# Weight transfers on a second queue, and nine feed ticks ahead of the first attention head instead of three

## The chip, the cores and the metric

One core of a Trainium2 chip. The metric is the device time of one execution in microseconds (us). A core has the engines TensorE (PE), VectorE (DVE), ScalarE (ACT), GpSimd (POOL) and SyncE (SP), which run their own instruction streams in order and wait for one another by semaphores, and DMA engines that move data between memory and the core. Both SP and ACT issue transfers in this kernel.

## The reference

Attention of 4 batches with 8 heads, 576 positions and 64 columns a head, and on its 2304 rows of 512 values two gated layers, one after the other, each with weights of 512x2048 and 2048x512:

```python
scores = scale * np.matmul(q, k.transpose(0, 1, 3, 2))
cum = np.cumsum(np.maximum(s, 0.0), axis=-1)
bias = -(cum[:, :, :, None] - cum[:, :, None, :])
scores = np.where(causal, -1000000000.0, scores + np.minimum(bias, 0.0))
attn = np.exp(scores - max); attn = attn / (sum + 1e-09)
x = np.matmul(attn, v)                    # to [2304, 512]
h = x @ w_in;  x = (h * np.clip(h + 3.0, 0.0, 6.0) / 6.0) @ w_out
h = x @ w_in2; out = (h * (1.0 / (1.0 + np.exp(-h)))) @ w_out2
```

The weights arrive as float64.

## The kernel before

**Heads and steps.** A head is 256 queries ("A") or the other 320 ("B") of one head of one batch; the work runs in slots, and a slot has the parts of up to three heads in flight: scores on PE, the masked maximum on DVE (L534), the exponential on ACT (L552), transposes on PE copied by ACT (`thA`, L120) and the product with v. Slots 0 to 8 have heads alone: the first block of rows is complete after eight heads. From slot 9 on each slot also has a step of the first gated layer: `first` (L260 to L262) multiplies a chunk of w_in, `gate_high` puts the gate through ACT (L272) and DVE (L273), `second` (L299 to L301) multiplies a chunk of w_out. "Gate n" below is the n-th L273 of DVE; the rows of the block itself come by `xh` (ACT, L725).

**Weights.** The first layer's weights are 32 chunks, i0, o0, i1, o1 to i15, o15. Each is loaded as raw 64-bit words, 128x1024 of 32 bits, 512 KB (L147, `rawi`, `rawo`), and turned into a pair of float32 pieces by seven operations: ACT L159 and L160, POOL L161, DVE L172 and L176 (the join), ACT L120 (`CAST wi` or `wo`, the high piece) and DVE L187 (the low piece). `Feed.tick` drives them as a pipeline: a tick loads one chunk, does L159 to L161 of the chunk loaded three ticks before, the join of the one before that, and the high and low piece of the one before that. Three ticks run ahead of the slots; slots 0 to 8 then get 0.4 tick each, later ones 2. `split_rows` builds rows for later heads and stores them with six transfers to `rows_d` (L365).

**Order.** A scheduler sets the order of instructions on each engine from the program; the engines keep that order. All transfers of the two queues take their completion semaphores in turn from one set of eight, in the program's order over both queues.

Of the kernel before, what the change touches and what calls it, by code (L numbers as in the profile page):

```python
# [11 lines left out]
I32 = mybir.dt.int32  # L12
# [15 lines left out]
def kernel(  # L28
# [15 lines left out]
    nc = tc.nc  # L44
# [85 lines left out]
    class Chunk:  # L130
        def __init__(self, kind, m, f):
            self.key = (kind, m, f)
            self.src = ((w1i, w1o), (w2i, w2o))[m][kind == "o"][f]
            self.nm = f"{kind}{m}_{f}"
            self.home = wpool, f"{kind}{f}"
# [2 lines left out]
            pool, tag = self.home  # L138
            return pool.tile(shape, dt, tag=tag, name=f"{name}{self.nm}")

        def load(self):
            if self.src.dtype == F32:
                self.val = self.place([P, DM], F32, "raw")
                nc.sync.dma_start(self.val, self.src)
            else:
                raw = self.place([P, 2 * DM], I32, "raw")
                nc.sync.dma_start(raw, self.src.bitcast(I32))  # L147
                words = raw.rearrange("p (n two) -> p n two", two=2)
                self.words = words[:, :, 0], words[:, :, 1]

# [38 lines left out]
    class Feed:  # L189


        def __init__(self, keys, hi_eng, lo_eng):
            self.ch = [Chunk(*k) for k in keys]
            self.hi_eng, self.lo_eng = hi_eng, lo_eng
            self.t = 0

        def done(self):
            return self.t >= len(self.ch) + 3 + 2

        def tick(self):  # L200
            n = len(self.ch)
            t = self.t - 3
            lo = self.lo_eng[t % len(self.lo_eng)] if 0 <= t - 2 < n else ""
            if lo:
                self.ch[t - 2].high(self.hi_eng[t % len(self.hi_eng)])
            if 0 <= t < n:
                self.ch[t].fields()
            if lo == "p":
                self.ch[t - 2].low(lo)
            if 0 <= t - 1 < n:  # L210
                self.ch[t - 1].join()
            if lo == "v":
                self.ch[t - 2].low(lo)
            if self.t < n:
                self.ch[self.t].load()
            self.t += 1


# [133 lines left out]
    def split_rows():  # L352

        def row(tag, name):
            return wpool.tile([BH, S], F32R, tag=tag, name=name)

        f = NF - 1
        hi, lo = row(f"i{f}", "cumh"), row(f"o{f}", "cuml")
        one, neg = row(f"i{NF // 2 - 2}", "one"), row(f"i{NF // 2 - 1}", "neg")
        nc.gpsimd.memset(f32(one), 1.0)  # L360
        nc.gpsimd.memset(f32(neg), -1.0)
        nc.scalar.copy(hi, crow)
        nc.vector.tensor_tensor(out=lo, in0=crow, in1=f32(hi), op=ALU.subtract)
        for r, t in enumerate((one, one, hi, lo, neg, neg)):
            nc.sync.dma_start(f32(rows_d[:, r, :]), f32(t))  # L365
# [347 lines left out]
    def split1(blk):  # L713

        n = sizes[blk][1]
        b, a, _ = blocks[blk][0]
        xhs, xls = [], []
        for c in range(NDC):
            xh = xpool.tile([P, n], F32R, tag=f"xh{c}", name=f"xh{blk}_{c}")
            xl = xpool.tile([P, n], F32R, tag=f"xl{c}", name=f"xl{blk}_{c}")  # L720
            srcs = [((xB if a else xA)[b, c], slice(0, T1))]
            if n > T1:
                srcs += [(xZ[c], slice(T1, n))]
            for src, o in srcs:
                nc.scalar.copy(xh[:, o], src)  # L725
                nc.vector.tensor_tensor(
                    out=xl[:, o], in0=src, in1=f32(xh[:, o]), op=ALU.subtract
                )
            xhs.append(xh)
            xls.append(xl)  # L730
        xsplit[blk] = [(xhs, xls)]
# [46 lines left out]
    feed = Feed([(kd, 0, f) for f in range(NF) for kd in "io"], "a", "v")  # L778
# [3 lines left out]
    def ticks(n):  # L782
        for _ in range(n):
            if not feed.done():
                feed.tick()
# [79 lines left out]
    def at(i):  # L865
        return heads[i] if 0 <= i < len(heads) else None


    loaded = 2
    for hd in heads[:loaded]:  # L870
        hd.load()
    ticks(3)
    for hd in heads[:loaded]:
        hd.load_cum()
    nc.sync.dma_start(pair_d, pairs)
    heads[0].places()
    k = 0
    p1 = p2 = None
    plan = [(True, False)] * (H + 1) + [(i < 55, True) for i in range(68)]
    nslot = 0  # L880
    for has_head, has_step in plan:
        cur = at(k) if has_head else None
        nx = at(k + 1) if has_head else None
        loads = []
        while has_head and loaded < len(heads) and loaded <= k + (
            2
        ):
            loads.append(heads[loaded])
            loaded += 1
        k += has_head and cur is not None  # L890
        tk = [0, 0, 0, 0]
        if not feed.done():
            rate = ((0.4,)*9+(2,))[min(nslot, len(((0.4,)*9+(2,))) - 1)]
            for i in range(4):
                feed_at += rate / 4
                tk[i] = int(feed_at)
                feed_at -= tk[i]
        slot(cur, p1, p2, nx, loads, has_step, tk)
        if nslot == 9:
            split_rows()  # L900
        p1, p2 = cur, p1
        nslot += 1
        if nslot == H + 1:
            p2.av_sum()
            p2 = None
            split1(0)
            turns["s"] = turns["s"][:1]
        if has_step and step in first_step[1:NB1]:
            blk = first_step.index(step)
            assert k - (cur is not None) >= (blk + 1) * H  # L910
            if p2:
                p2.av_sum()
                p2 = None
            if blk == NB1 - 1:
                cx.close()
                xpool = cx.enter_context(
                    tc.tile_pool(name="xlast", bufs=1, side="right", reuse_waits="tile")
                )
            split1(blk)
            if blk == NB1 - 1:  # L920
                break
# [70 lines left out]
    feed = Feed([("o", 1, f) for f in range(NF)], "a", "v")  # L992
# [293 lines left out]
```

## Time and profile before

| what | value |
|---|---|
| median of 3 runs | 1000.1 us (998.52 to 1000.47) |
| profiled execution | 1000.54 us, its span 998.8 us, granted PE clock 0.995 |
| busy share of the span | PE 97%, PEld 89%, DVE 74%, ACT 51%, POOL 32% |

The span is the time from the first to the last instruction in the trace; the shares are over the whole of it. The slots with heads alone end at 43 us and the last gate of the first sixteen steps is at 154 us, so the stretch that the change touches is the first sixth of the span.

### The profile page before, as it was taken

What the parts mean: (1) busy time and instruction counts of PE and PEld (TensorE: products, weight loads), DVE (VectorE), ACT (ScalarE), POOL (GpSimd) and SP (SyncE); (2) the same over time, 40 slices, a digit from 0 to 9 for tenths busy, and PEclk for the clock granted to TensorE, in tenths of its full rate; (3) what the DMA queues carried; (4) which work ended last, traced back from release to release, by engine and by line L of the source; (5) the groups of instructions that cost most, each with busy time, mean ns of one, the idle gap of its engine ahead of it and who ended that gap; (6) DMA issues with size and microseconds to landing.
All of it is one profiled execution on the core that took longest, in us unless ns stands there. A gap on an engine that the chain in (4) does not pass through costs nothing.

```text
span 998.8 us, 17929 instructions
## 1 busy us (share of the span) xinstructions
PE 970.8 (97%) x6268; PEld 891.6 (89%) x6268; DVE 737.9 (74%) x1757; ACT 511.0 (51%) x1177; POOL 317.2 (32%) x323
## 2 busy tenths in 40 slices
PE   8899989999999999999999999999999999999997
PEld 5789979999999999999997877899988989889996
DVE  6899998888789888988866799887574434743343
ACT  6898554555455555555446656564443323432332
POOL 4457853443333443434425566532000000000000
PEclk9999999999999999999999999999999999999999
DMA  5796112312222223222215957434354233442421
GB/s 174 225 302 198 47 40 67 92 46 63 83 77 75 71 59 92 60 64 80 60 39 186 392 212 237 163 116 190 133 195 169 77 145 110 167 154 76 148 74 64
DMA packets 54419, 125.41 MB, mean 126 GB/s; under 512 B 12332, under 2 KB 34076, under 8 KB 51000
## 3 DMA queue, kind: packets, MB, share of 16 engines
q1 hardware_dynamic: 53880, 123.60, 37.3%
q8 instruction: 50, 0.82, 0.3%
q10 hardware_dynamic: 448, 0.66, 0.2%
q14 instruction: 41, 0.34, 0.1%
HBM read 99.52 MB, written 24.69 MB: 124 GB/s over the span
## 4 chain that ended last, share of the span: by engine, by line
PE 70%; DVE 11%; DMA 8%; issue 4%; POOL 4%; SPq 3%; ACT 1%; POOLq 0%; DVEq 0%; ACTq 0%
PE a L1083 6%; PE a L1084 6%; PE a L1085 6%; PE h L1066 5%; PE h L1068 5%; PE h L1067 5%; PE ph L260 4%; PE ph L261 4%; PE ph L262 4%; PE acc L299 4%; PE acc L300 4%; PE acc L301 4%; PE poB L672 4%; DMA rawi<-in_w1i_dram 3%; POOL rawo L161 2%
## 5 line engine op out<-in xcount | busy, mean ns | idle before, releaser
L260 PE MATMUL ph<-xh,wi 128*128 128x256 f32 (+1 forms) x512 | 154.1, 303 | 3.2 <-DVE g L273 3.1
L300 PE MATMUL acc<-gl,wo 128*128 128x256 f32 (+1 forms) x512 | 151.1, 297 | 2.4 <-DVE gl L280 2.4
L261 PE MATMUL ph<-xl,wi 128*128 128x256 f32 (+1 forms) x512 | 151.6, 296 | 0.0
L262 PE MATMUL ph<-xh,wi 128*128 128x256 f32 (+1 forms) x512 | 151.3, 296 | 0.0
L301 PE MATMUL acc<-gh,wo 128*128 128x256 f32 (+1 forms) x512 | 149.8, 294 | 0.0
L1125 ACT ACTIVATE gh<-h 128x384 fp32r<-128x384 f32 x96 | 50.3, 524 | 185.4 <-DVE h L1133 185.3
L299 PE MATMUL acc<-gh,wo 128*128 128x256 f32 (+1 forms) x512 | 143.8, 297 | 0.0
L1083 PE MATMUL a<-wo,gh 128*128 128x512 f32 x288 | 113.5, 394 | 1.4 <-ACT gh L1125 0.9
L1084 PE MATMUL a<-wo,gh 128*128 128x512 f32 x288 | 113.1, 393 | 0.0
L260 PEld LDWEIGHTS ph<-xh,wi 128*128 128x128 f32 x512 | 97.4, 190 | 8.9 <-DVE g L273 2.5
L300 PEld LDWEIGHTS acc<-gl,wo 128*128 128x128 f32 x512 | 96.4, 188 | 6.4 <-DVE gl L280 3.5
L262 PEld LDWEIGHTS ph<-xh,wi 128*128 128x128 f32 x512 | 97.6, 191 | 3.0
L261 PEld LDWEIGHTS ph<-xl,wi 128*128 128x128 f32 x512 | 97.5, 190 | 3.2
L301 PEld LDWEIGHTS acc<-gh,wo 128*128 128x128 f32 x512 | 96.5, 189 | 3.3
L299 PEld LDWEIGHTS acc<-gh,wo 128*128 128x128 f32 x512 | 95.6, 189 | 3.4
L161 POOL TENSOR_SCALAR rawi<-rawi 128x512 int32<-128x512 f32 x32 | 70.0, 2188 | 74.1 <-ACT magi L160 48.4
L1085 PE MATMUL a<-wo,gl 128*128 128x512 f32 x288 | 90.0, 392 | 0.0
L161 POOL TENSOR_SCALAR rawo<-rawo 128x512 int32<-128x512 f32 x32 | 74.5, 2329 | 48.0 <-ACT mago L160 46.3
L1127 DVE TENSOR_TENSOR gl<-h,gh 128x384 fp32r<-128x384 f32 x96 | 53.8, 560 | 39.9 <-ACT h L1126 38.2
L114 POOL TENSOR_SCALAR gh<-g 128x512 fp32r<-128x512 f32 x68 | 50.6, 745 | 92.6 <-DVE g L273 77.4
L1133 DVE TENSOR_TENSOR h<-h,u 128x384 f32<-128x384 f32 x72 | 40.1, 557 | 53.5 <-PE h L1068 53.2
L1066 PE MATMUL h<-x0t,w 128*128 128x384 f32 x192 | 64.9, 338 | 0.7 <-DVE u L1133 0.7
(220 smaller groups left out, 2554.6 us busy)
## 6 DMA issues: line engine op xcount, KB each, us to landing
w<-w_d SPq DMA_DIRECT2D x18, 1792.0 KB
w_d<-w SPq DMA_DIRECT2D x8, 1792.0 KB
k2B<-in_kT_dram SPq DMA_DIRECT2D x64, 144.0 KB
rawi<-in_w1i_dram SPq DMA_DIRECT2D x16, 512.0 KB
rawo<-in_w1o_dram SPq DMA_DIRECT2D x16, 512.0 KB
rawi<-in_w2i_dram SPq DMA_DIRECT2D x16, 512.0 KB
rawo<-in_w2o_dram SPq DMA_DIRECT2D x16, 512.0 KB
q2B<-in_qT_dram SPq DMA_DIRECT2D x64, 80.0 KB
```

What stands on the lines that cost most here:

```text
L161: nc.gpsimd.tensor_scalar(out=high, in0=f32(high), scalar1=0.0, scalar2=float(SIGN), op0=ALU.is_lt, op1=ALU.mult,)
L260: nc.tensor.matmul(o, wih[:, cs], xh[c], start=c == 0, stop=False)
L261: nc.tensor.matmul(o, wih[:, cs], xl[c], start=False, stop=False)
L262: nc.tensor.matmul(o, wil[:, cs], xh[c], start=False, stop=c == NDC - 1)
L299: nc.tensor.matmul(a, woh[:, cs], gh[:, jj, :], start=b0, stop=False)
L300: nc.tensor.matmul(a, woh[:, cs], gl[:, jj, :], start=False, stop=False)
L301: nc.tensor.matmul(a, wol[:, cs], gh[:, jj, :], start=False, stop=b1)
L1066: nc.tensor.matmul(ps, w[:, 0, cs], xh[:, c, :], start=c == 0, stop=False)
L1083: nc.tensor.matmul(accs[t], gh[:, k, cs], woh, start=b0, stop=False)
L1084: nc.tensor.matmul(accs[t], gh[:, k, cs], wol, start=False, stop=False)
L1085: nc.tensor.matmul(accs[t], gl[:, k, cs], woh, start=False, stop=b1)
L1127: nc.vector.tensor_tensor(out=gl[:, i, o], in0=g, in1=f32(gh[:, i, o]), op=ALU.subtract)
```

## The change

`Chunk.load` takes the queue that issues its transfer, and `Feed` keeps one. It is ACT's queue from the start to the end of slot 8, and SP's after that. The three ticks ahead of the slots move ahead of the loads of the first two heads, and three more ticks follow the store of `pair_d`. `split_rows` comes after slot 7 instead of slot 9. Lines behind the edit stand 1 to 4 further down in the changed kernel.

```diff
--- before.py
+++ after.py
@@ -138,13 +138,13 @@
             pool, tag = self.home
             return pool.tile(shape, dt, tag=tag, name=f"{name}{self.nm}")
 
-        def load(self):
+        def load(self, queue=nc.sync):
             if self.src.dtype == F32:
                 self.val = self.place([P, DM], F32, "raw")
-                nc.sync.dma_start(self.val, self.src)
+                queue.dma_start(self.val, self.src)
             else:
                 raw = self.place([P, 2 * DM], I32, "raw")
-                nc.sync.dma_start(raw, self.src.bitcast(I32))
+                queue.dma_start(raw, self.src.bitcast(I32))
                 words = raw.rearrange("p (n two) -> p n two", two=2)
                 self.words = words[:, :, 0], words[:, :, 1]
 
@@ -193,6 +193,7 @@
             self.ch = [Chunk(*k) for k in keys]
             self.hi_eng, self.lo_eng = hi_eng, lo_eng
             self.t = 0
+            self.queue = nc.sync
 
         def done(self):
             return self.t >= len(self.ch) + 3 + 2
@@ -212,7 +213,7 @@
             if lo == "v":
                 self.ch[t - 2].low(lo)
             if self.t < n:
-                self.ch[self.t].load()
+                self.ch[self.t].load(self.queue)
             self.t += 1
 
 
@@ -867,12 +868,14 @@
 
 
     loaded = 2
+    feed.queue = nc.scalar
+    ticks(3)
     for hd in heads[:loaded]:
         hd.load()
-    ticks(3)
     for hd in heads[:loaded]:
         hd.load_cum()
     nc.sync.dma_start(pair_d, pairs)
+    ticks(3)
     heads[0].places()
     k = 0
     p1 = p2 = None
@@ -896,11 +899,12 @@
                 tk[i] = int(feed_at)
                 feed_at -= tk[i]
         slot(cur, p1, p2, nx, loads, has_step, tk)
-        if nslot == 9:
+        if nslot == 7:
             split_rows()
         p1, p2 = cur, p1
         nslot += 1
         if nslot == H + 1:
+            feed.queue = nc.sync
             p2.av_sum()
             p2 = None
             split1(0)
```

What the scheduler makes of it shows at three places. The first is ACT's start, up to the first exponential (`pb0A_0`). Before:

```order
L350 ACT_TABLE_LOAD
L350 COPY pairs<-orow 32x256
L362 CAST cumh<-orow 32x576
L159 ACTIVATE rawi_0_171<-rawi_0_171 128x512
L160 ACTIVATE magi_0_257<-rawi_0_171 128x512
L159 ACTIVATE rawo_0_173<-rawo_0_173 128x512
L160 ACTIVATE mago_0_354<-rawo_0_173 128x512
L159 ACTIVATE rawi_1_175<-rawi_1_175 128x512
L160 ACTIVATE magi_1_450<-rawi_1_175 128x512
L552 ACTIVATE pb0A_0_181,sums_127<-pb0A_0_181,mxA_0_180 128x128
```

And now, where nine transfers are issued by ACT (the L147 rows):

```order
L147 DMA rawi_0_163<-in_w1i_dram 128x1024
L147 DMA rawo_0_165<-in_w1o_dram 128x1024
L147 DMA rawi_1_167<-in_w1i_dram 128x1024
L351 ACT_TABLE_LOAD
L351 COPY pairs<-orow 32x256
L147 DMA rawo_1_184<-in_w1o_dram 128x1024
L159 ACTIVATE rawi_0_163<-rawi_0_163 128x512
L160 ACTIVATE magi_0_180<-rawi_0_163 128x512
L147 DMA rawi_2_192<-in_w1i_dram 128x1024
L159 ACTIVATE rawo_0_165<-rawo_0_165 128x512
L160 ACTIVATE mago_0_186<-rawo_0_165 128x512
L147 DMA rawo_2_203<-in_w1o_dram 128x1024
```

Further on in the same stretch, from ACT's last issue to the first exponential:

```order
L147 DMA rawi_4_490<-in_w1i_dram 128x1024
L120 CAST wi_0_194<-magi_0_180 128x512
L363 CAST cumh<-orow 32x576
L159 ACTIVATE rawi_2_192<-rawi_2_192 128x512
L160 ACTIVATE mago_1_284<-rawo_1_184 128x512
L159 ACTIVATE rawo_2_203<-rawo_2_203 128x512
L120 CAST wo_0_282<-mago_0_186 128x512
L159 ACTIVATE rawi_3_291<-rawi_3_291 128x512
L120 CAST wi_1_384<-magi_1_196 128x512
L159 ACTIVATE rawo_3_393<-rawo_3_393 128x512
L160 ACTIVATE magi_2_386<-rawi_2_192 128x512
L553 ACTIVATE pb0A_0_206,sums_127<-pb0A_0_206,mxA_0_205 128x128
```

Before its first exponential ACT had three chunks' L159 and L160 each. Now it has the L159 of eight chunks, five L160, three casts and nine issues; the rows between these two pieces are the transfers o2, i3 and o3, L159 and L160 of i1, and the L159 of o1.

The second is SP's start. Before, rows 8 to 18, the raw chunks i0, o0, i1, and what SP issues behind them up to the first transfer of the fourth head (`inA_3`):

```order
L147 DMA rawi_0_171<-in_w1i_dram 128x1024
L147 DMA rawo_0_173<-in_w1o_dram 128x1024
L147 DMA rawi_1_175<-in_w1i_dram 128x1024
L423 DMA inA_0_163<-pairs 2x1x512
L423 DMA inA_1_167<-pairs 2x1x512
L875 DMA pair_d<-pairs 32x1024
L413 DMA inA_2_191<-in_qT_dram 64x256
L414 DMA inA_2_191<-in_kT_dram 64x256
L403 DMA inA_2_191<-in_v_dram 128x128
L423 DMA inA_2_191<-pairs 2x1x512
L413 DMA inA_3_218<-in_qT_dram 64x256
```

Now, from the second head's transfers to the same place:

```order
L414 DMA inA_1_173<-in_qT_dram 64x256
L415 DMA inA_1_173<-in_kT_dram 64x256
L404 DMA inA_1_173<-in_v_dram 128x128
L424 DMA inA_0_169<-pairs 2x1x512
L424 DMA inA_1_173<-pairs 2x1x512
L877 DMA pair_d<-pairs 32x1024
L414 DMA inA_2_216<-in_qT_dram 64x256
L415 DMA inA_2_216<-in_kT_dram 64x256
L404 DMA inA_2_216<-in_v_dram 128x128
L424 DMA inA_2_216<-pairs 2x1x512
L414 DMA inA_3_243<-in_qT_dram 64x256
```

The three raw loads have left SP, and the transfers of a head follow each other. In the program's order over both queues the first transfer of `inA_2` is the eighth after ACT's o2, that of `inA_3` the eighth after o3.

The third is the tenth chunk, o4. SP before, from the ninth head:

```order
L413 DMA inA_0_405<-in_qT_dram 64x256
L414 DMA inA_0_405<-in_kT_dram 64x256
L403 DMA inA_0_405<-in_v_dram 128x128
L423 DMA inA_0_405<-pair_d 2x512
L413 DMA inA_1_442<-in_qT_dram 64x256
L414 DMA inA_1_442<-in_kT_dram 64x256
L403 DMA inA_1_442<-in_v_dram 128x128
L147 DMA rawo_2_457<-in_w1o_dram 128x1024
```

SP now, from the last transfer of the tenth head:

```order
L424 DMA inA_1_475<-pair_d 2x512
L366 DMA rows_d<-one 32x576 x2
L366 DMA rows_d<-cumh 32x576
L366 DMA rows_d<-cuml 32x576
L366 DMA rows_d<-neg 32x576 x2
L414 DMA inA_2_533<-in_qT_dram 64x256
L415 DMA inA_2_533<-in_kT_dram 64x256
L404 DMA inA_2_533<-in_v_dram 128x128
L424 DMA inA_2_533<-pair_d 2x512
L147 DMA rawo_4_585<-in_w1o_dram 128x1024
```

And ACT now, around the first use of o4:

```order
L553 ACTIVATE pb0A_6_412,sums_131<-pb0A_6_412,mxA_6_411 128x128
L553 ACTIVATE pb1A_6_413,sums_131<-pb1A_6_413,mxA_6_411 128x256
L553 ACTIVATE pb0A_7_445,sums_133<-pb0A_7_445,mxA_7_444 128x128
L553 ACTIVATE pb1A_7_446,sums_133<-pb1A_7_446,mxA_7_444 128x256
L159 ACTIVATE rawo_4_585<-rawo_4_585 128x512
L160 ACTIVATE mago_4_693<-rawo_4_585 128x512
L120 COPY thA_4_400<-pt0A_4_396 128x384
L726 CAST xh_1_557<-xA_1_382 128x256
L120 COPY thA_5_433<-pt0A_5_429 128x384
L159 ACTIVATE rawi_5_628<-rawi_5_628 128x512
```

SP had a raw load for every one or two heads there. Now the six stores of `rows_d` and a whole eleventh head stand ahead of o4, the first raw chunk that SP loads, and on ACT the L159 of o4 stands ahead of what remains for the first gate: the copies `thA_4` and `thA_5` and the rows `xh_1`.

Counted from the same orders, the operations of conversion on either side of the gates:

| engine, lines | where | before | now |
|---|---|---|---|
| ACT, L159 | ahead of gate 0 | 8 | 21 |
| DVE, L172 L176 L187 | ahead of gate 0 | 20 | 44 |
| DVE, the same | gate 0 to gate 7 | 30 | 31 |
| DVE, the same | gate 7 to gate 11 | 24 | 21 |
| DVE, the same | gate 11 to gate 16 | 22 | 0 |

The matmuls between gate 0 and gate 16 are the same in both.

## Rows read from the trace of the kernel before

**Rows 1.** Windows: us, busy us (instructions) of each engine, clock, DMA share, GB/s.
```profile
12.76:42.41 29.65, 24.71 (x173) 20.00 (x172) 26.28 (x105) 25.24 (x80) 12.87 (x7) 1.00 0.63 180
43.10:80.80 37.70, 35.48 (x270) 33.60 (x271) 36.30 (x111) 35.12 (x87) 23.40 (x12) 0.95 0.93 290
80.80:111.00 30.20, 27.95 (x231) 26.67 (x231) 29.17 (x70) 22.73 (x55) 22.12 (x14) 1.00 0.44 138
111.00:154.30 43.30, 38.26 (x291) 35.60 (x291) 42.59 (x97) 24.38 (x58) 25.81 (x24) 0.96 0.17 44
150.00:200.00 50.00, 49.80 (x410) 49.17 (x411) 42.99 (x121) 25.00 (x65) 19.51 (x27) 1.00 0.27 79
```

**Rows 2.** Chain of work in the first 40 us: start, us, what.
```profile
5.81 5.79 DMA rawi<-in_w1i_dram
11.61 0.48 SPq L413
...
28.91 4.46 DMA rawo<-in_w1o_dram
```

**Rows 3.** Timeline of ACT up to gate 0: start, us, operation.
```profile
38.84 0.61 ACT L120 CAST wo<-mago 128x512 fp32r<-128x512 f32 x1
39.35 0.47 ACT L120 COPY thA<-pt0A 128x384 f32<-128x384 f32 x1
39.72 0.41 ACT L725 CAST xh<-xA 128x256 fp32r<-128x256 f32 x1
40.02 0.69 ACT L159 ACTIVATE rawo<-rawo 128x512 int32<-128x512 uint32 x1
40.60 0.66 ACT L160 ACTIVATE mago<-rawo 128x512 f32<-128x512 f32 x1
...
41.52 0.41 ACT L552 ACTIVATE pb0A<-pb0A,mxA 128x128 f32<-128x128 f32 x1
41.91 0.50 ACT L552 ACTIVATE pb1A<-pb1A,mxA 128x256 f32<-128x256 f32 x1
42.41 0.46 ACT L272 ACTIVATE g<-ph,half 128x256 f32<-128x256 f32 x1
```

**Rows 4.** Timeline of DVE, gate 0 and gate 16.
```profile
43.11 0.41 DVE L273 SCALAR_TENSOR_TENSOR g<-g,ph 128x256 f32<-128x256 f32 x1
...
154.29 0.69 DVE L273 SCALAR_TENSOR_TENSOR g<-g,ph 128x512 f32<-128x512 f32 x1 [0.27 <-ACT g L272]
```

**Rows 5.** Timeline of ACT up to the first exponential, and the chunk o1.
```profile
4.65 0.40 ACT L350 COPY pairs<-orow 32x256 f32<-32x256 f32 x1 [2.65 <-DVE orow L345]
...
12.20 0.65 ACT L160 ACTIVATE magi<-rawi 128x512 f32<-128x512 f32 x1
12.76 0.39 ACT L552 ACTIVATE pb0A<-pb0A,mxA 128x128 f32<-128x128 f32 x1
...
19.50 0.70 ACT L159 ACTIVATE rawo<-rawo 128x512 int32<-128x512 uint32 x1 [0.55 <-DMA rawo<-in_w1o_dram]
```

**Rows 6.** Timeline of SP's queue, issues.
```profile
15.90 0.43 SPq L147 DMA_DIRECT2D rawo<-in_w1o_dram  x1
...
16.71 0.48 SPq L413 DMA_DIRECT2D inA<-in_qT_dram  x1
...
18.84 0.47 SPq L413 DMA_DIRECT2D inA<-in_qT_dram  x1
...
35.41 0.78 SPq L365 DMA_DIRECT2D rows_d<-one  x2
```

**Rows 7.** Timeline of ACT near the end, a transfer that ACT issues.
```profile
991.49 0.39 ACTq L1107 DMA_DIRECT2D out_dram<-o  x1
```

**Rows 8.** Groups of DVE between gate 0 and gate 16, two of conversion's six.
```profile
L187 DVE TENSOR_TENSOR wi<-magi,wi 128x512 fp32r<-128x512 f32 x13 | 10.8, 831 | 0.0
...
L172 DVE SCALAR_TENSOR_TENSOR magi<-magi,rawi 128x512 int32<-128x512 int32 x12 | 8.2, 684 | 0.3 <-POOL rawi L161 0.2
```

## The prediction

> **What bounds the kernel now.** I read the shares first: PE is busy 97% of the span, so an edit far from it is worth nothing unless it makes PE wait. Then the windows, to see where PE does not run at its own rate [rows 1]. From 150 to 200 us PE does 410 matmuls in 50 us, 8.2 a us, and is busy all through: that is its rate when everything is there. From gate 0 to gate 16 it does 270 + 231 + 291 = 792 matmuls in 111.2 us [rows 1, 4]; at 8.2 a us they would take 96.6. So 14.6 us could be won there, and the reader sees by whom it is lost: DVE is busy 36.3 of 37.7, 29.2 of 30.2 and 42.6 of 43.3 us [rows 1]. DVE bounds the steps, and a good part of its work there is conversion of weights. Ahead of gate 0 nothing is full: between the first exponential and gate 0 ACT is busy 25.2 of 29.65 us and DVE 26.3 [rows 1]; ACT and DVE hand the heads to each other. Last I read the chain of the first 40 us, which is transfers: SP's issue at 11.61 us follows the landing of i1, issued at 5.81, and the next gap follows o2, issued at 28.91 and 4.46 us under way [rows 2]. In the order shown above, the issue at 11.61 (`inA_3`) is the eighth transfer after i1. So an issue waits until the transfer eight before it, whose semaphore it reuses, has landed; the issues behind it on its engine wait with it.
>
> **The change part by part: the delay of gate 0.** It loads nine chunks early on ACT's queue, converts more of them ahead of gate 0, and leaves less conversion for later. I follow ACT, with occupancies taken from start to start [rows 3]: L159 0.58 us, L160 0.56 (12.20 to 12.76) [rows 5], a cast 0.51, `thA` 0.37, `xh` 0.30, the exponentials 0.39 and 0.50.
>
> First exponential. ACT's copy of `pairs` starts at 4.65 us [rows 5] and stays near there, since it waits for `irow`, still SP's first transfer; three issues in front of it make it 5.1 at its end. Behind it come six issues, 13 of L159 and L160, three casts and the `cumh` cast. An issue by ACT shows once, 0.39 us [rows 7]; SP's take 0.43 for these very transfers [rows 6], which I take: 2.6. With 13 x 0.57 = 7.4, 3 x 0.51 = 1.5 and 0.6 the sum is 12.1, so the first exponential starts at about 17.3 instead of 12.76 us, 17.5 with a short wait of the i4 issue for i2. That is 4.7 us late.
>
> From there to the L159 of o4 stand 16 exponentials (7.1), five of L159 and L160 (2.8), six casts (3.1), four `thA` (1.5) and an `xh` (0.3): 14.8 us, so ACT reaches o4 at 32.3 us if DVE and PE keep up.
>
> When o4 is there depends on SP. Its first transfer of `inA_2` waits for o2 by the rule of eight. ACT issues o2 behind two issues and four conversion operations, 5.1 + 0.9 + 2.3 = 8.3 us; landing takes 3.6 us (15.90 issued, L159 at 19.50) [rows 5, 6] to 4.46 [rows 2], so `inA_2` starts at 12.3. Heads `inA_2` and `inA_3` are done at about 17.4, held a little by o3 and i4. The next six take 2.13 us each (16.71 to 18.84) [rows 6]: 30.2. The six stores to `rows_d`, which the earlier `split_rows` puts here, take 6 x 0.39 = 2.3 (two in 0.78) [rows 6]: 32.5. The eleventh head, 2.13: 34.7. Only then is o4 issued, to land at 38.3 to 39.2. **ACT stands still for about 6.5 us, from 32.3 to 39**, and behind it wait the next exponentials and the `thA` copies and `xh` of the first block's last heads, which gate 0 needs. DVE and PE have nothing of their own to go on with.
>
> From o4 to gate 0 ACT has ten exponentials (4.5), twelve L159 (7.0), six L160 (3.4), five casts (2.6), six `thA` (2.2) and three `xh` (0.9): 20.5 us, so gate 0 is at 39 + 20.5 = 59.5 on ACT, 42.41 before [rows 3]. A second count agrees: from o4 to i10, whose L159 stands just ahead of the gate, twelve chunks of 512 KB and some 0.8 MB of heads are 7.1 MB, 24.5 us at the 290 GB/s of the densest window [rows 1]; 34.7 + 24.5 is 59.2. **I take a delay of 17 us.** Bounds: no stall at all and ACT full, 17.5 + 14.8 + 20.5 = 52.8, or +10.4; the last 20.5 us at the 0.85 of the stretch of before [rows 1], 63.1, or +20.7.
>
> **What is given back.** Conversion on DVE between gate 0 and gate 16 falls from 76 operations to 52. The cheapest of the six groups is 0.684 us a piece, the dearest 0.831 [rows 8]; with the middle, 0.75, 24 of them are 18 us of DVE. But PE cannot go under 96.6 us, so at most 14.6 come back. And it matters where they are missing: to gate 11 DVE has 52 instead of 54, which is 1.5 us of a stretch that DVE fills. From gate 11 to gate 16 it has none instead of 22, 16.5 us less; DVE's 42.6 fall to 26.1, PE becomes the bound there, and its 291 matmuls take 35.5 us instead of 43.3: 7.8. **I take 9.3 us back**, bounds 1.5 + 0 (ACT or the heads hold those last steps) and 14.6. Past gate 16 PE is full in both and runs the same matmuls: nothing further changes hands.
>
> The rest costs nothing. The queue itself moves bytes and does not add any; the earlier `split_rows` is priced above; `places` and the idle matmuls at the start are the same.
>
> What the second queue is worth by itself: SP loses six raw issues ahead of the ninth head, 0.43 us each [rows 6], 2.6 us, and ACT gets them. Behind this stands a sentence of the Trainium skill ("DMA: Bandwidth & Descriptors", section "Issuing engines are not separate DMA queues"): transfers started by several engines share the same DMA engines, and this saves only the time a sequencer takes to issue them. By it the change would be worth some 2.6 us and no more; whether these transfers overlap more than before, no row here shows yet, and the long delay above is of order and semaphores, not of bandwidth.
>
> **The sum.** 998.8 + 17 - 9.3 = 1006.5 for the span; with the 1.7 us that lie around it (1000.54 against 998.8), 1008.2. The profiled execution is 0.4 above the median of the runs, so the runs should show about 1007.5.
>
> **Rivals.** *Faster.* If o4 and the chunks behind it land before ACT comes to them, gate 0 is at 52.8 (+10.4), and if DVE's relief then reaches every step, 14.6 come back: -4.2, or 996. The point that decides is SP's issue of o4: ahead of 28 us, against my 34.7. For it: three of the waits in the chain are for landings, and raw loads spread over two queues could land sooner than 4.46 us. Against it: the six stores and eleven heads stand ahead of o4 whatever the landing. *Even.* Gate 0 at 57 to 59.5 and nearly the whole 14.6 given back: within 2 us, about 1000. For it: conversion that is done early is work that DVE need not do later, and DVE bounds these steps by 96% and more [rows 1]. Against it: the missing work is at the end, more than PE can use. *Nothing given back.* The heads with steps pace the stretch past gate 11, through ACT and POOL or the transfers of `q2A` and `k2A` that now stand behind the raw loads on SP: +17 less 1.5, about 1015.5. Against it: ACT is busy 24.4 of 43.3 us there [rows 1]. *The issue time alone.* The scheduled order delays nothing because the chain of transfers shrinks by as much as ACT gains: -2.6, about 997.5. Against it: 21 chunks' L159 instead of 8 stand ahead of the gate.
>
> **How the numbers follow.** The forecast, 1007.5, has 0.6, and its own range is 1002.5 to 1013 (17 less 14.6 is +2.4; 20.7 less 7.8 is +12.9). Faster by the rival with o4 early 0.1, by issue time alone 0.05; even 0.15; nothing given back 0.1. The measurement tells about 0.2%, 2 us, from no change. Of the forecast's low end a little falls to the other sides: faster 0.16, same 0.17, slower 0.67. The range from 997 to 1014 leaves out the rival with o4 early and the one with nothing given back, 0.2 together.
>
> **What the changed profile would show.** The first exponential at about 17.5 us; SP's first transfer of `inA_2` at 12 to 13 us; ACT idle from about 32 to 39 us until o4 lands; gate 0 on DVE at about 60 us; no conversion after gate 11, PE full from there, and gate 16 some 8 us later than 154.29 [rows 4]. The forecast is wrong if ACT reaches o4 with o4 landed, if gate 0 comes before 57.7 us on DVE (43.1 + 14.6, where delay and the most that can come back are equal), or if PE still waits for DVE between gate 11 and gate 16.

## The result and the profile after

The changed kernel takes 1010.6 us (median of 4 runs, 1008.2 to 1012.0) against 1000.3 of the kernel before in the same comparison: a ratio of 1.0093, 95% interval 1.0069 to 1.0117. It is slower, as forecast (1007.5), by 10.3 us instead of 7.4, and inside the range. The profiled execution has a span of 1010.2 us, 11.4 more than before's 998.8.

The page of the changed kernel, busy time of each engine over the span, and the granted clock of PE in 40 slices of 25 us, in tenths:

```profile
PE 984.0 (97%) x6268; PEld 904.0 (89%) x6268; DVE 736.3 (73%) x1757; ACT 511.6 (51%) x1177; POOL 311.6 (31%) x323
...
PEclk7759999999999999999999999999999999999999
```

PE has the same 6268 instructions and 13 us more busy time; the first three slices say why: the clock was granted at 0.7, 0.7 and 0.5 there. The windows of the changed kernel, cut at its own first exponential, its L159 of o4, its gate 0 (on ACT, then on DVE), gates 7, 11 and 16, answer to [rows 1]:

```profile
19.67:42.31 22.64, 21.12 (x93) 17.16 (x94) 19.95 (x71) 15.99 (x50) 10.31 (x5) 0.59 0.42 117
42.31:65.28 22.97, 19.11 (x94) 16.41 (x94) 17.65 (x61) 20.55 (x53) 12.04 (x6) 0.71 0.97 332
66.16:104.11 37.95, 36.34 (x270) 34.76 (x271) 36.44 (x107) 32.21 (x81) 23.86 (x12) 0.92 0.44 144
104.11:132.12 28.01, 27.34 (x230) 26.37 (x229) 27.82 (x74) 17.67 (x43) 19.11 (x14) 1.00 0.20 57
132.12:164.48 32.36, 32.36 (x278) 32.19 (x277) 22.28 (x56) 14.77 (x36) 8.93 (x15) 1.00 0.14 39
```

In time these windows hold 270 + 230 + 278 = 778 matmuls between gate 0 and gate 16, where the kernel before has 792: the matmuls are the same, but 228 instead of 216 run ahead of gate 0.

The gates on DVE, which answer to [rows 4]:

```profile
66.16 0.41 DVE L274 SCALAR_TENSOR_TENSOR g<-g,ph 128x256 f32<-128x256 f32 x1
...
164.48 0.69 DVE L274 SCALAR_TENSOR_TENSOR g<-g,ph 128x512 f32<-128x512 f32 x1 [0.81 <-ACT g L273]
```

Gate 0 is 66.16 - 43.11 = 23.1 us late. From gate 0 to gate 16 it takes 98.3 us instead of 111.2, so 12.9 come back; behind gate 16 it is 1.2 us more (845.7 against 844.5). 23.1 - 12.9 + 1.2 is the 11.4. Most of what comes back does so where it was forecast, from gate 11 to gate 16: 32.4 us instead of 43.3, with PE busy for all of it and DVE for 22.3 instead of 42.6.

Now how gate 0 came to be so late. ACT's timeline, answering to [rows 3, 5]; behind an operation stand the idle time ahead of it and what ended it:

```profile
6.08 0.40 ACT L351 COPY pairs<-orow 32x256 f32<-32x256 f32 x1 [2.63 <-DVE orow L346]
...
13.07 0.62 ACT L120 CAST wi<-magi 128x512 fp32r<-128x512 f32 x1 [1.04 <-DMA rawi<-in_w1i_dram]
...
16.36 0.62 ACT L120 CAST wo<-mago 128x512 fp32r<-128x512 f32 x1 [0.41 <-DVE mago L176]
...
19.67 0.39 ACT L553 ACTIVATE pb0A<-pb0A,mxA 128x128 f32<-128x128 f32 x1
...
33.53 0.62 ACT L120 CAST wo<-mago 128x512 fp32r<-128x512 f32 x1 [1.76 <-DVE sums L562]
...
37.31 0.41 ACT L726 CAST xh<-xA 128x256 fp32r<-128x256 f32 x1 [1.09 <-DVE xA L122]
...
39.91 0.40 ACT L553 ACTIVATE pb0A<-pb0A,mxA 128x128 f32<-128x128 f32 x1 [1.16 <-DVE xtA L695]
...
42.31 0.68 ACT L159 ACTIVATE rawo<-rawo 128x512 int32<-128x512 uint32 x1
...
65.28 0.46 ACT L273 ACTIVATE g<-ph,half 128x256 f32<-128x256 f32 x1
```

The first exponential is at 19.67 us, 2.2 later than forecast. `irow`, issued at 0.73 us in both kernels, landed later beside the raw loads, so the copy of `pairs` starts at 6.08 instead of 4.65. Then ACT waited for landings and for DVE's joins. The wait ahead of 13.07 is that of an issue, by the rule of eight: i4 goes out when i2 has landed, as the chain of work and ACT's timeline have it:

```profile
6.52 6.10 DMA rawi<-in_w1i_dram
...
12.64 0.33 ACTq L147 DMA_DIRECT2D rawi<-in_w1i_dram  x1
```

From the first exponential to o4 it took 22.6 us instead of the 14.8 that ACT's own work would need. The operation ahead of the row at 42.31 ends at 42.18 and o4 lands at 42.28, so ACT waits for it for some 0.1 us. The stall of 6.5 us for o4 does not exist, because ACT comes 10 us later than forecast; o4 itself lands 3 us later than forecast. ACT loses its time before, waiting for DVE (33.53, 37.31, 39.91). In that window DVE is busy 19.95 and PE 21.12 of 22.64 us, and PE has a granted clock of 0.59. PE's timeline shows what that means:

```profile
14.95 0.77 PE L513 MATMUL ps0A<-inA 66*128 66x128 f32 x2 [3.03 <-DMA inA<-pairs]
...
20.29 0.44 PE L581 MATMUL pt0A<-ident,pb0A 128*128 128x128 f32 x1 [2.44 <-ACT pb0A L553]
...
23.10 0.64 PE L513 MATMUL ps0A<-inA 66*128 66x128 f32 x2
...
42.91 0.38 PE L513 MATMUL ps0A<-inA 66*128 66x128 f32 x2
...
50.02 0.49 PE L513 MATMUL ps0A<-inA 66*128 66x128 f32 x2 [1.75 <-DVE mxA L535]
```

PE stood still for 3.0 us ahead of its first scores, whose data came late, and for 2.4 us ahead of the first transposes, which waited for the late exponential. Two scores of 66x128 take 0.64 us at 23.10 and 0.38 at 42.91, 0.38 too in the kernel before (at 12.15). The windows of the experiments below have the clock at 0.50, which is 1.2 GHz, behind such pauses.

From o4 on the chain of work runs over landings, as the prediction had it. SP's two issues first, then the chain from 38 us:

```profile
14.12 0.54 SPq L414 DMA_DIRECT2D inA<-in_qT_dram  x1
...
38.43 0.35 SPq L147 DMA_DIRECT2D rawo<-in_w1o_dram  x1
```

```profile
38.43 3.85 DMA rawo<-in_w1o_dram
...
43.71 5.71 DMA rawi<-in_w1i_dram
...
49.44 0.33 SPq L147
...
50.21 4.16 DMA q2A<-in_qT_dram
```

`inA_2` starts at 14.12 (forecast 12 to 13), o4 is issued at 38.43 (34.7) and lands at 42.28; then i6 is under way for 5.71 us before the issue at 49.44, the eighth behind it, goes, and `q2A` for 4.16; the profile puts ACT's next wait, which ends at 54.41, down to it. Ahead of o4 no raw load had been issued since i4 at 12.64 us, and behind that gap work runs short. The changed kernel from 35 to 50 us:

```profile
35.00:50.00 15.00, 11.79 (x77) 9.63 (x75) 9.14 (x39) 10.01 (x29) 4.97 (x3) 0.89 0.82 252
```

DVE is busy 9.14 and ACT 10.01 of 15 us. In the version below with three chunks on ACT's queue the same stretch has 11.62 and 12.94.

### The profile page after: what moved, and what is told of

It reads as the page before. It is cut to its first block, busy times and chain, and to the rows that moved or that the text cites. A ratio compares the mean times of both kernels' runs of the same rounds, so it can differ in the third digit from the quotient of the medians.

```text
span 1010.2 us, 17956 instructions
## 1 busy us (share of the span) xinstructions
PE 984.0 (97%) x6268; PEld 904.0 (89%) x6268; DVE 736.3 (73%) x1757; ACT 511.6 (51%) x1177; POOL 311.6 (31%) x323
## 4 chain that ended last, share of the span: by engine, by line
PE 74%; DVE 12%; DMA 5%; issue 4%; POOL 3%; ACT 1%; SPq 1%; ACTq 0%; POOLq 0%; DVEq 0%
PE a L1087 6%; PE a L1088 6%; PE a L1089 6%; PE h L1070 5%; PE h L1072 5%; PE h L1071 5%; PE ph L261 5%; PE ph L262 5%; PE ph L263 5%; PE acc L301 5%; PE acc L300 5%; PE acc L302 5%; PE poB L673 3%; POOL rawo L161 2%; DMA rawi<-in_w2i_dram 2%
## 5 line engine op out<-in xcount | busy, mean ns | idle before, releaser
L161 POOL TENSOR_SCALAR rawi<-rawi 128x512 int32<-128x512 f32 x32 | 67.4, 2107 | 80.1 <-ACT magi L160 53.2
L161 POOL TENSOR_SCALAR rawo<-rawo 128x512 int32<-128x512 f32 x32 | 72.7, 2275 | 43.1 <-ACT mago L160 40.6
```

The source lines that it names most:

```text
L161: nc.gpsimd.tensor_scalar(out=high, in0=f32(high), scalar1=0.0, scalar2=float(SIGN), op0=ALU.is_lt, op1=ALU.mult,)
```

## The experiments

Three theories stood to be told apart. "Early conversion" is the prediction's: conversion ahead of gate 0 is the delay. "Queue" puts it on ACT's queue: its issues, and an SP that runs ahead with the heads and leaves the raw loads for later. "Clock" is new from the trace: the pause of PE drops its clock, and the heads then run at half of it. Each kernel was timed in five rounds against the kernel before. A table of all stands behind them. Every edit also moves the scheduler's order on all engines, so a ratio is that of the edit with its order. Six ticks, not the nine of the title, run ahead of the slots in the changed kernel; the other three of the nine transfers on ACT's queue come from slots 0 to 8.

**The extra ticks alone.** The kernel before with

```diff
     nc.sync.dma_start(pair_d, pairs)
+    ticks(3)
```

> The kernel before with nothing but the three more ticks behind the store of pair_d; all weights stay on SP's queue. Its order has 38 conversion operations on DVE ahead of gate 0 (before 20, changed kernel 44). Theory 'early conversion' (the added work ahead of gate 0 on DVE and ACT is the delay): gate 0 on DVE at 53 to 60 us and a time of 1003 to 1009. Theory 'queue' (ACT's issues and nine raw transfers ahead of the heads' own data make the delay): gate 0 within 3 us of 43.1 and a time of 998 to 1001. Theory 'clock' (the pause between the idle matmuls and the first scores drops PE's clock): no low clock here, 998 to 1002.

Measured: 1.0030 (1.0014 to 1.0046), gate 0 at 58.3 us, 97.9 us on to gate 16. "Early conversion" has its gate 0, and the clock was low here too (0.77 up to gate 0), against what "clock" expected. But 13.3 of the 15.2 us of delay came back (97.9 instead of 111.2): a late gate 0 by itself costs little, here 0.3%.

**ACT's queue taken away.** The changed kernel without

```diff
-    feed.queue = nc.scalar
     ticks(3)
```

> The changed kernel with SP's queue for all weights: the first three ticks stay ahead of the heads' loads, the extra ticks and split_rows after slot 7 stay. Its order has 31 conversion operations on DVE ahead of gate 0. 'Early conversion': gate 0 at 50 to 55 us, time 1001 to 1006. 'Queue': most of the loss is gone, 998 to 1002. 'Clock': the three raw loads still stand ahead of the heads' data, so the first scores are late, the clock falls as in the changed kernel (0.6 to 0.9 in the first 40 us), and the time stays at 1007 to 1011.

Measured: 0.9993 (0.9981 to 1.0006), gate 0 at 49.7 us. The whole loss is gone with that line. The first clock dip is there (0.50 from 20 to 25 us), but it is shorter (0.62 from 25 to 30 us, then 1.00) and has no second behind it up to gate 0.

**ACT's queue without the extra ticks.** The changed kernel with

```diff
     nc.sync.dma_start(pair_d, pairs)
-    ticks(3)
...
-        if nslot == 7:
+        if nslot == 9:
             split_rows()
```

> The changed kernel without the three extra ticks and with split_rows back after slot 9: left are ACT's queue and the first three ticks ahead of the heads' loads. Its order has six raw loads on ACT's queue and 33 conversion operations on DVE ahead of gate 0. 'Early conversion': gate 0 at 51 to 57 us, time 1002 to 1007. 'Queue': nearly the whole loss stays, 1007 to 1012. 'Clock': a low clock in the first 40 us as in the changed kernel, and 1007 to 1012.

Measured: 1.0080 (1.0068 to 1.0092), gate 0 at 60.0 us. That is as "queue" and "clock" have it: the loss without the extra ticks.

**A longer bridge at the start.** The changed kernel with

```diff
-    keep_clock(34, busy[:, :512])
+    keep_clock(48, busy[:, :512])
```

> The changed kernel with 48 idle matmuls at the start instead of 34, so that PE runs on (about 0.3 us each) until the first scores, which came at 14.95 us after a pause of 3.0. Nothing else in the program is changed; the scheduler's order moves a little (44 conversion operations on DVE ahead of gate 0, as before the edit). 'Clock': the granted clock stays at 1.0 from the start to gate 0, gate 0 comes before 60 us instead of 66.2, and the time falls to 1000 to 1005. 'Early conversion': DVE is busy 88% and ACT 71% between the first exponential and o4 already, so gate 0 stays at 62 to 66 us and the time at 1007 to 1011 even with the full clock.

Measured: 1.0073 (1.0061 to 1.0086), gate 0 at 64.0 us. It does not test the clock, since the clock fell all the same (0.75 up to gate 0); PE's timeline of this kernel:

```profile
20.00 0.45 PE L581 MATMUL pt0A<-ident,pb0A 128*128 128x128 f32 x1 [3.20 <-ACT pb0A L553]
```

The second pause, for the first exponential, was enough. So a better test was made.

**Idle matmuls up to gate 0.** The changed kernel with 54 idle matmuls at the start, and

```diff
-            keep_clock(3, heads_of(p1.prob[1]))
+            keep_clock(9, heads_of(p1.prob[1]))
```

> The changed kernel with more idle matmuls on PE: 54 instead of 34 at the start and 9 instead of 3 behind each head's transposes, so that PE has no long pause ahead of gate 0. The bridge alone (48 at the start) let the granted clock fall anyway, since PE paused again from 16 to 19 us for the first exponential. Theory 'clock' (PE at half its clock bounds the heads from 20 to 38 us and again from 50 us): the granted clock stays at 0.9 to 1.0 up to gate 0, gate 0 comes at 55 to 61 us instead of 66.2, and the time falls to 1000 to 1005. Theory 'queue' (ACT's issues, and SP's order behind the semaphores of its transfers, set the delay): gate 0 stays at 63 us or later, time 1006 to 1012.

Measured: 1.0083 (1.0068 to 1.0097), gate 0 at 62.6 us. Four windows of this kernel, and the same four of the changed kernel:

```profile
25.00:30.00 5.00, 5.00 (x44) 4.36 (x41) 4.81 (x14) 3.34 (x8) 3.27 (x2) 1.00 0.33 93
30.00:35.00 5.00, 3.24 (x23) 2.36 (x21) 4.32 (x14) 2.23 (x6) 2.37 (x2) 1.00 0.46 120
50.00:55.00 5.00, 4.38 (x23) 3.55 (x23) 4.96 (x16) 4.31 (x11) 0.76 (x2) 0.66 1.00 307
55.00:60.00 5.00, 3.81 (x17) 3.09 (x15) 2.80 (x12) 4.76 (x13) 3.45 (x2) 0.50 1.01 383
```

```profile
25.00:30.00 5.00, 5.00 (x21) 4.12 (x21) 5.00 (x21) 3.76 (x12) 3.73 (x2) 0.50 0.34 97
30.00:35.00 5.00, 5.00 (x22) 4.20 (x21) 5.00 (x17) 3.14 (x9) 2.22 (x2) 0.50 0.34 90
50.00:55.00 5.00, 4.67 (x19) 3.85 (x19) 5.00 (x17) 4.15 (x11) 1.10 (x1) 0.69 0.97 310
55.00:60.00 5.00, 3.78 (x18) 3.02 (x16) 2.94 (x12) 5.00 (x16) 3.95 (x2) 0.50 0.87 293
```

From 25 to 35 us the clock is now full, and PE gets through 67 matmuls (idle ones among them) instead of 43. Gate 0 comes 3.6 us earlier, between what the two theories gave, and the ratio does not differ from that of the changed kernel within the intervals. From 30 to 35 us PE and ACT are busy 3.24 and 2.23 of 5 us and DVE 4.32, and from 50 us the clock is low again. So the first clock dip is not the cause; it is worth some 4 us of gate 0. The second dip is still in this run.

**Three chunks on ACT's queue.** The changed kernel with

```diff
     feed.queue = nc.scalar
     ticks(3)
+    feed.queue = nc.sync
     for hd in heads[:loaded]:
         hd.load()
```

> The changed kernel with ACT's queue for the first three chunks alone; the three extra ticks and all later chunks are on SP's queue, split_rows after slot 7. Its order has 33 conversion operations on DVE ahead of gate 0 and raw loads on SP between the heads. With all chunks on SP the loss was gone (0.9993), with nine on ACT it is 1.0093. If it is the chunks four to nine on ACT's queue, which let SP run ahead with the heads and leave the later raw loads in one burst, this comes out as the version on SP: gate 0 at 48 to 53 us, 999 to 1003. If ACT's queue as such costs it (the first three landing in front of irow and the heads' data), 1005 to 1010.

Measured: 1.0004 (0.9990 to 1.0018), gate 0 at 54.9 us, 2 us behind the forecast. The one edit takes 0.9% away, so the loss hangs on the chunks four to nine on ACT's queue, not on the first three. How it comes about is not shown by that, since this edit also leaves 33 conversion operations ahead of gate 0 instead of 44. Its windows, and those of the version with six on ACT and no extra ticks, which has the same 33 (and differs in the place of split_rows as well):

```profile
25.00:30.00 5.00, 5.00 (x27) 4.11 (x27) 5.00 (x21) 3.57 (x10) 2.67 (x3) 0.64 0.51 170
30.00:35.00 5.00, 3.10 (x22) 2.32 (x21) 4.90 (x13) 2.62 (x8) 2.50 (x1) 1.00 0.76 226
50.00:55.00 5.00, 4.56 (x24) 3.83 (x24) 4.81 (x17) 5.00 (x14) 1.91 (x1) 0.75 1.02 313
55.00:60.00 5.00, 5.00 (x26) 4.85 (x26) 3.86 (x10) 5.00 (x14) 2.89 (x2) 0.57 0.75 245
```

```profile
25.00:30.00 5.00, 5.00 (x21) 3.99 (x21) 3.70 (x15) 2.61 (x10) 0.00 (x0) 0.50 0.35 99
30.00:35.00 5.00, 5.00 (x27) 4.46 (x25) 2.32 (x12) 1.26 (x3) 0.00 (x0) 0.60 0.45 107
50.00:55.00 5.00, 3.91 (x17) 3.15 (x16) 4.68 (x19) 5.00 (x15) 2.12 (x2) 0.61 1.00 331
55.00:60.00 5.00, 4.01 (x17) 3.64 (x18) 2.89 (x9) 4.12 (x11) 3.20 (x2) 0.50 1.02 381
```

Look at the DMA share and at DVE. With three on ACT, raw loads go out between the heads, the transfers are busy 0.51 and 0.76 of the time from 25 to 35 us, and DVE has work for 9.9 of 10 us. With six on ACT, SP brings heads alone up to 32.8 us (its first raw issue), transfers are busy 0.35 and 0.45, POOL does nothing, DVE 6.0 of 10 us; then from 50 to 60 us the transfers are full (1.00 and 1.02, up to 381 GB/s) and PE does 17 matmuls in 5 us at a clock of 0.61 and 0.50. Full transfers at that time are no mark of the slow kernels: the kernel before has 1.03 and 1.01 there and PE does 84 matmuls in the 10 us.

The time at low clock does not order the kernels either. The first 100 us of the changed kernel with idle matmuls (1.0083), then of this one (1.0004):

```profile
0.00:100.00 100.00, 89.10 (x555) 71.38 (x556) 82.77 (x247) 78.58 (x196) 58.46 (x42) 0.90 0.67 217
0.00:100.00 100.00, 88.07 (x547) 74.72 (x548) 82.45 (x252) 79.88 (x201) 54.29 (x41) 0.86 0.70 219
```

The slower of the two has the higher mean clock, 0.90 against 0.86.

**split_rows after slot 9.** The changed kernel with

```diff
-        if nslot == 7:
+        if nslot == 9:
             split_rows()
```

> The changed kernel with split_rows back after slot 9: ACT's queue, the first three ticks ahead of the heads and the three extra ticks stay. On SP o4 now stands ahead of the six rows_d stores. If the stores ahead of o4 carry a part of the delay, gate 0 comes 2 to 6 us before 66.2 and the time is 1004 to 1008. If the delay is of the nine early chunks on ACT's queue (conversion ahead of the heads, then all later raw loads in one burst), nothing changes: 1008 to 1012.

Measured: 1.0122 (1.0097 to 1.0146), gate 0 at 68.6 us. ACT's row of o4:

```profile
39.31 0.66 ACT L159 ACTIVATE rawo<-rawo 128x512 int32<-128x512 uint32 x1 [1.09 <-DMA rawo<-in_w1o_dram]
```

ACT stands for o4 here, and o4 comes 3.0 us earlier (39.31 for 42.31), yet gate 0 is 2.4 us later. So an earlier o4 does not bring gate 0 forward. What the stores cost is not separated: the first scores came behind a pause of 4.8 us in this run, and the clock was at 0.50 up to 45 us.

**split_rows after slot 7, alone.** The kernel before with the reverse of that edit.

> The kernel before with split_rows after slot 7 instead of slot 9 and nothing else. The six stores of 0.39 us each come 2.3 us ahead of two heads' loads and some raw chunks on SP. All theories so far put this part at nothing or little: 999 to 1003, gate 0 within 3 us of 43.1.

Measured: 1.0084 (1.0062 to 1.0106), against what every theory said. Gate 0 is where it was (42.6 us); the loss is behind it. Its window from gate 0 to gate 7, and DVE's gates 14 and 15:

```profile
42.65:88.66 46.01, 43.35 (x286) 40.64 (x285) 39.35 (x125) 37.65 (x96) 24.06 (x12) 0.83 0.82 256
```

```profile
144.02 0.68 DVE L273 SCALAR_TENSOR_TENSOR g<-g,ph 128x512 f32<-128x512 f32 x1
...
162.48 0.67 DVE L273 SCALAR_TENSOR_TENSOR g<-g,ph 128x512 f32<-128x512 f32 x1
```

Gate 0 to gate 7 takes 46.0 us instead of 37.7 [rows 1], with PE busy at a clock of 0.83 instead of 0.95, and gates 14 and 15 lie 18.5 us apart instead of 11.9. So moving this one call makes the steps slower, by 8.3 us up to gate 7 and 5.2 from there to gate 16 (the expectation of the last run below names the second part alone). Whether the order on DVE or the clock does it, and which of the moved instructions, was not settled. In the other pair, the changed kernel with the call at 7 and at 9, it made no difference that can be told.

**The first three chunks, alone.** The kernel before with the first three ticks on ACT's queue and ahead of the heads' loads, all else on SP.

> The kernel before with only its first three ticks changed: they go over ACT's queue and stand ahead of the heads' loads; all later weights are on SP's queue, no extra ticks, split_rows after slot 9. Its order has 19 conversion operations on DVE ahead of gate 0 (before 20). 'Queue', where the loss is in the six further transfers that ACT issues later: no loss, 998 to 1002. 'Queue', where the loss is in raw transfers ahead of the heads' own data: the first scores come at 13 to 15 us instead of 11.4, gate 0 2 to 4 us late, 1002 to 1005. 'Clock': as the second, if the pause of PE in front of the first scores is over 2 us, with a low clock behind it and 1003 to 1008.

Measured: 1.0044 (1.0030 to 1.0058). Neither reading of "queue" has it right: the first scores and gate 0 are on time (11.3 and 42.9 us), the clock is full up to it, and the loss is again between gate 0 and gate 16 (116.8 us). Up to gate 0 and on to gate 7, and last the kernel before up to its gate 0:

```profile
0.00:42.92 42.92, 36.09 (x216) 25.38 (x216) 31.56 (x114) 31.26 (x87) 18.42 (x25) 1.00 0.65 187
42.92:83.15 40.23, 36.48 (x272) 33.78 (x273) 37.66 (x114) 35.91 (x89) 23.77 (x12) 0.96 0.86 271
...
0.00:43.11 43.11, 36.13 (x216) 25.38 (x216) 31.55 (x117) 31.78 (x89) 19.92 (x25) 1.00 0.62 184
```

PE, DVE and ACT have nearly the same work done by gate 0 as in the kernel before; the steps are then slower, 40.2 us for 37.7.

**Fill on the version with SP's queue.** ACT's queue taken away, 40 idle matmuls at the start, 9 behind each head's transposes.

> The changed kernel with SP's queue for all weights, as in the run that took ACT's queue away (gate 0 at 49.7 us, low clock from 15 to 28 us, 0.9993 of before), and with more idle matmuls: 40 at the start, 9 behind each head's transposes. 'Clock': the granted clock stays up, gate 0 comes at 45 to 48 us, and the kernel is 2 to 5 us faster than before, 995 to 999. 'Queue': the clock cost nothing here, DVE and ACT pace the heads, and the time stays at 1000 to 1002.

Measured: 0.9971 (0.9959 to 0.9982), 996.8 us: the only kernel here that beats the one before beyond its interval. Its windows from 50 us:

```profile
50.00:55.00 5.00, 5.00 (x45) 4.92 (x44) 5.00 (x15) 5.00 (x14) 2.92 (x2) 1.00 1.02 327
55.00:60.00 5.00, 4.97 (x41) 4.62 (x40) 5.00 (x19) 5.00 (x15) 2.10 (x3) 1.00 1.05 290
```

Full clock, transfers full, DVE full, and 86 matmuls in 10 us where the changed kernel had 37 (and the kernel before 84).

**Its control.** The kernel before with the same fill.

> The kernel before with more idle matmuls, 40 instead of 34 at the start and 9 instead of 3 behind each head's transposes, and nothing else: the control for the version on SP's queue with the same fill (0.9971). Its granted clock was 1.0 up to 40 us already. If the gain of that version is the early conversion kept at full clock, this one stays at 999 to 1003; if the fill alone brings it (the scheduler's order moves too: 27 conversion operations on DVE ahead of gate 0 instead of 20), 995 to 998.

Measured: 1.0016 (1.0002 to 1.0031). The fill alone gains nothing. As a control it is not clean: its clock was lower (0.86 up to gate 0, against 1.00 in the kernel before and 0.97 in the version on SP's queue), and its gate 0 is at 54.2 us. So that the gain of 0.9971 is early conversion kept at full clock fits, and is not shown.

**The same with split_rows after slot 9.**

> The version on SP's queue with fill, and split_rows back after slot 9: first three ticks ahead of the heads' loads, three extra ticks, all on SP, 40 and 9 idle matmuls. split_rows after slot 7 alone cost 0.8% in the kernel before, though its loss arose between gate 7 and gate 16. If that loss is in this version too, 990 to 995; if it belongs to that one order only, 995 to 999 as with the split after slot 7.

Measured: 0.9996 (0.9983 to 1.0008). The better place of the call in the kernel before is the worse one here by 0.25%, so its worth hangs on the order that it meets.

All kernels, sorted by the conversion operations that their order has on DVE ahead of gate 0 (times in us from the profiled execution, which for single kernels lies up to 3.3 us from the median):

| kernel | conversion ahead | gate 0 | clock to gate 0 | gate 0 to 16 | behind gate 16 | ratio |
|---|---|---|---|---|---|---|
| before, split at 7 | 18 | 42.6 | 1.00 | 124.8 | 841.8 | 1.0084 |
| before, first three on ACT | 19 | 42.9 | 1.00 | 116.8 | 844.5 | 1.0044 |
| before | 20 | 43.1 | 1.00 | 111.2 | 844.5 | 1 |
| before, fill | 27 | 54.2 | 0.86 | 103.8 | 844.9 | 1.0016 |
| on SP, fill | 29 | 48.8 | 0.97 | 102.1 | 843.2 | 0.9971 |
| on SP | 31 | 49.7 | 0.86 | 102.1 | 844.2 | 0.9993 |
| six on ACT, no extra ticks | 33 | 60.0 | 0.76 | 102.3 | 845.0 | 1.0080 |
| three on ACT | 33 | 54.9 | 0.82 | 101.5 | 845.4 | 1.0004 |
| on SP, fill, split at 9 | 34 | 52.5 | 0.88 | 101.6 | 844.6 | 0.9996 |
| before, extra ticks | 38 | 58.3 | 0.77 | 97.9 | 846.6 | 1.0030 |
| changed, fill | 41 | 62.6 | 0.88 | 101.6 | 842.0 | 1.0083 |
| changed | 44 | 66.2 | 0.71 | 98.3 | 845.7 | 1.0093 |
| changed, 48 at the start | 44 | 64.0 | 0.75 | 94.7 | 845.7 | 1.0073 |
| changed, split at 9 | 45 | 68.6 | 0.66 | 98.8 | 840.7 | 1.0122 |

Three things stand in it. Gate 0 goes up with the conversion ahead of it, by (66.2 - 43.1) / 24 = 1.0 us an operation from before to changed, but not with that alone: at 33 and 34 operations it is at 60.0 with six on ACT, at 54.9 and at 52.5. What comes back does not grow as far: with 27 to 34 operations ahead the stretch takes 101.5 to 103.8 us instead of 111.2, with 38 to 45 it takes 94.7 to 101.6. With 27 to 34 ahead the two are about even or better (0.9971 to 1.0016), six on ACT excepted; with 41 and more they are not. Behind gate 16 the same work takes 840.7 to 846.6 us, so a few us between two single rows say little.

Last, "early conversion" is not excluded as the way in which nine chunks on ACT's queue cost their time. In two of the kernels with all weights on SP and no added fill gate 0 goes from 49.7 us with 31 operations to 58.3 with 38, 1.2 us each; carried on to 44, an estimate from these two, it would be at 65.7, and the changed kernel has it at 66.2. Only the version with six on ACT has gate 0 late without more conversion ahead.

## Why the prediction was right, and where it was off

The direction, the place and the shape of the sum held: gate 0 late, part of it given back, most of that from gate 11 to gate 16, PE full there, and nothing changed behind it (1.2 us). That the time came within 3 us is in part luck: the delay was 6.1 us more than forecast and 3.6 us more came back. (The sum as it stands, 1000.1 + 17 - 9.3, gives 1007.8, not 1007.5.)

- **The delay of gate 0** was mis-sized: 17 forecast, bound 20.7, measured 23.1. The bound was passed on the way to o4, which ACT reached at 42.3 instead of 39 and for which the bound had no slack; from o4 on, 23.0 us is inside its 24.1. PE's clock was taken as unchanged: the fill, which gives back most of the clock up to 50 us, brings gate 0 3.6 us forward, a delay of 19.5.
- **The step that failed is "ACT stands still for about 6.5 us, from 32.3 to 39".** I let ACT run ahead on its own work "if DVE and PE keep up". They did not: DVE had 44 conversions to do ahead of gate 0, PE ran at a clock of 0.59, and ACT was free for o4 only at 42.2. On SP, o4 landed at 42.28 instead of 39, so the two ways met within 0.1 us. The leg to o4 came out near because the time was lost anyway, to waits for DVE, and that is luck. With the call at 9 o4 came 3.0 us earlier, and gate 0 did not.
- **The first exponential**: 17.5 forecast, 19.67 measured; the copy of `pairs` did not "stay near there", since `irow` landed later beside the raw loads.
- **From o4 to gate 0**: 20.5 forecast, 23.0 measured (42.31 to 65.28), inside the bound. ACT is busy 20.55 us of it, as its count had it, and the transfers' share is 0.97, as the count by bytes had it; which of the two sets the time is not shown.
- **Given back**: 9.3 forecast, 12.9 measured, inside the bound of 14.6. The term from gate 11 to gate 16 was 7.8 and became 10.9: PE's rate there was 278 matmuls in 32.36 us, 8.6 a us, not the 8.2 that I took, and 278 stand there instead of 291, since 12 more ran ahead of gate 0. So 96.6 us is no floor for PE: the version with 48 idle matmuls at the start took 94.7.
- **The queue by itself**, which I had at 2.6 us in its favour, is where the loss hangs: 1.0093 with nine chunks on ACT, 1.0004 with three, 0.9993 with none. The rule of eight is part of how: SP's heads follow one another without raw loads between them, and no raw load at all is issued from 12.64 us (i4, on ACT) to 38.43 (o4, on SP). Behind that gap DVE and ACT ran short of work from 35 to 50 us. I priced the late raw loads in bytes and did not see the sparse stretch ahead of them, nor PE's low clock. The sentence of the Trainium skill ("DMA: Bandwidth & Descriptors", section "Issuing engines are not separate DMA queues") fits what three on ACT show: the second queue brought no time that can be told, not even the issue time of three loads, 1.3 us.

Open stays how the loss at nine chunks divides between the conversion ahead of gate 0, the sparse stretch and the clock dip from 50 us; the fill took away only the first dip. Open too is why split_rows after slot 7 costs 0.8% in one order and nothing in others.

## What to carry to other kernels

Work that is done ahead to relieve a later stretch is worth its price only up to a point: here about ten of the 24 conversion operations that were moved. When transfers of two engines share one set of completion semaphores, moving some to the other engine also moves the waits of those that stay, so look at what the old queue now does early and what it leaves for later. A hand chain along one engine needs the share of the others beside it at each stretch, and the clock that a new pause of PE will bring.

## What the runs showed of the hardware

In the changed kernel the granted clock fell in a pause of PE of 3.0 us and, with another pause of 2.4 us behind it, stayed at 0.50 (1.2 GHz) until about 38 us: the windows have 0.50 from 15 to 35 us and 0.68 from 35 to 40. From 25 to 35 us PE was busy throughout, at two scores in 0.64 us instead of 0.38. From 50 us, behind a wait of 1.75 us, the clock fell to 0.50 again. It did so too in the versions with six on ACT and with the extra ticks, but not in the two fastest. It also fell (0.50 from 45 to 50 us) in the version on SP with fill and the call at 9, which is as fast as the kernel before (0.9996). A load of 72 KB (`irow`), issued at 0.73 us in both kernels, let its reader start at 4.21 us with three raw loads issued by ACT beside it, and at 2.64 without. Moving a single call without a byte more or less (split_rows) was worth 0.8%, with gate 0 unmoved.
